# Ordering the q work behind the value product's eviction, and the ranks of three batches in an ordinary PSUM bank

## The chip, the cores and the metric

The kernel runs on one core of one Trainium2 chip. The metric is the device time of one launch in microseconds; there is one span and one granted TensorE clock to look at.

## The reference, cut to what matters

Three stages follow each other. The first is attention over 4 batches, 8 heads, 576 positions of 64 values: `scores = q k^T / 8` under a causal mask, softmax, times `v`; a second term reads a memory matrix with `phi(q) = max(q,0) + min(exp(q),1)`, divides by its own norm, and a gate per head mixes the two. The result is cast into rows `x` of 512 values, 2304 of them.

The second stage is a mixture of 8 experts. For each row an argmax over 8 logits picks the expert, softmax gives its weight `gate_w`, and an output gate is a sigmoid:

```
h = max(x[mask] @ w1[e], 0); out[mask] = gate_w * eom * (h @ w2[e])
```

The third stage is a dense layer, `max(x @ w_in, 0)**2 @ w_out`, on all 2304 rows.

## The kernel before

**Attention.** The two heads of a pair are handled together, so there are 16 pairs (4 batches of 4). A pair goes through four stages, each a lane in one loop: *prep* (load q and k, split them into a high and a low part, DMA the parts into stacked tiles `q2`, `k2`, `qlz`), *front* (scores into PSUM, row maximum `negm` on VectorE, exponential `a` on ScalarE), *back* (TensorE transposes of `a` into `pt`, copies into `aTs`, the memory read `pm`, the value product into `pva` and `pvb`), and *end* (transposes of the value product into `ppt`, the mix `tl` and `xb`, store, transposes `pxt`, gate logits `plg`). One turn of the loop, here called a step, runs the end of one pair, the back of the next, the front of the one after, and the prep of the one after that. So a step is about one pair's work on each engine, and four pairs are in flight.

The order on each engine is not written out. The program is traced lane by lane, and a scheduler with a timeline of its own then picks, engine by engine, which ready instruction comes next. Each engine executes its instructions in that order; what one needs from another is a semaphore wait. The context `tc.issue_after(ins)` adds only an ordering rule for that scheduler: what is traced inside it is placed behind `ins` on the same engine. It adds no wait on the chip by itself.

The lines around the change: L171 evicts PSUM tiles, among them `pvs<-pva` on ScalarE, remembered as `c.value`. L188 casts `kh`, L198 to L200 compute `qh`, `ex`, `rq` on ScalarE from the loaded tile `qraw` (two buffers), L201 computes `ql` and L226 `qpad` on VectorE. L275 is the row maximum, L278 the exponential. Transposes have line L76. The score of the last 64 rows goes through `psl`, a PSUM tile of two banks of which there is one buffer (`c.wide`); other PSUM tiles come from a pool of six banks (`c.bank`).

**Routing.** After a batch's last pair, `route_batch` computes on VectorE which expert each row takes (`oh`), on TensorE each row's rank among the rows of its expert (`prank`), on VectorE again the gate's softmax (`zs`, `eo`, `sp`) and from the ranks a block and an offset (`rblk`, `roff`). The first three batches are routed inside the attention loop, the last one inside the expert stage. When three batches are known, `route_early` fills the first expert slots, so that the first rows and weights can be fetched while the last pairs of attention still run.

**Experts and dense layer** run behind it in an order that is largely written out, and are not touched.

Of the kernel before, what the change touches and what calls it, by code (L numbers as in the profile page):

```python
# [12 lines left out]
I32 = mybir.dt.int32  # L13
U32 = mybir.dt.uint32
AF = mybir.ActivationFunctionType
ALU = mybir.AluOpType
AX = mybir.AxisListType
# [4 lines left out]
B, H, S, D = 4, 8, 576, 64  # L22
# [3 lines left out]
NB = 5  # L26
# [110 lines left out]
def attention(tc, c, q, k, v, x_dram, pools):  # L137
    nc = tc.nc
# [34 lines left out]
    def pair(b, hp, lgT):  # L173
# [6 lines left out]
        def load(nm, src, pool, nb):  # L180
            t = pool.tile([P, S], F32, tag=nm + "raw", name=nm + "raw", bufs=nb)
            nc.sync.dma_start(out=t, in_=src[b, hp])
            return t

        ks = load("k", k, fr, 3)
        qs = load("q", q, fr, 2)
# [7 lines left out]
        ql = fr.tile([P, S], F32R, tag="ql", name="ql", bufs=1)  # L194
        ex = fr.tile([P, S], F32, tag="ex", name="ex", bufs=1)
        rq = fr.tile([P, S], F32, tag="rq", name="rq", bufs=1)
        with tc.issue_after(c.value.ins) if c.value and b == 0 else nullcontext():
            nc.scalar.mul(qh, qs, 0.125)  # L198
        nc.scalar.activation(ex, qs, AF.Exp)
        nc.scalar.activation(rq, qs, AF.Relu)  # L200
        nc.vector.scalar_tensor_tensor(out=ql, in0=qs, scalar=0.125, in1=qh.bitcast(F32), op0=ALU.mult, op1=ALU.subtract)  # L201
        stacked = b or hp >= NPLAIN

# [237 lines left out]

    order = list(pairs())
    gens = [pair(*o) for o in order]
    n = len(gens)

# [71 lines left out]
def route_batch(tc, c, b, wk):  # L517
    nc = tc.nc
    cs = slice(b * NB, (b + 1) * NB)
    sh = (P, NB, E)  # L520
    lg, lo = c.lg[:, cs, 0:E], c.lg[:, cs, E:2 * E]
    oh = c.oh[:, cs]

    def t3(name):
        return wk.tile([P, NB, E], F32, tag=name, name=name, bufs=1)

    def t2(name, dt=F32):
        return wk.tile([P, NB], dt, tag=name, name=name, bufs=1)

    mx, m2, zs, so = t2("mx"), t2("m2"), t2("zs"), t2("so")  # L530
    dd, eo = t3("dd"), t3("eo")
    tt = c.tt[b % 2]
    tx = tt[:, :, 0:E]
    nc.scalar.activation(eo, lo, AF.Exp, scale=-1.0)
    nc.vector.tensor_reduce(out=mx, in_=lg, axis=AX.X, op=ALU.max)
    mxb = mx.unsqueeze(2).to_broadcast(sh)
    yield "f"
    nc.vector.tensor_tensor(out=tx, in0=lg, in1=mxb, op=ALU.is_equal)
    nc.vector.tensor_sub(dd, lg, mxb)
    yield "f"  # L540
    nc.vector.tensor_mul(tx, tx, c.edv)
    yield "f"
    nc.scalar.activation(dd, dd, AF.Exp)
    nc.vector.tensor_reduce(out=m2, in_=tt, axis=AX.X, op=ALU.max)
    yield "f"
    nc.vector.tensor_tensor(out=oh, in0=tx, in1=m2.unsqueeze(2).to_broadcast(sh), op=ALU.is_equal)
    yield "q"
    pr = c.wide("prank")
    pv = pr[:, 0:NB * E]
    ohf = oh.rearrange("p j e -> p (j e)")  # L550
    nc.tensor.matmul(pv, lhsT=c.ones, rhs=c.cum[:, b:b + 1].to_broadcast((P, NB, E)), start=True, stop=False)
    nc.tensor.matmul(pv, lhsT=c.tri, rhs=ohf, start=False, stop=False)
    for j in range(1, NB):
        nc.tensor.matmul(pr[:, j * E:NB * E], lhsT=c.ones, rhs=ohf[:, 0:(NB - j) * E], start=False, stop=j == NB - 1)
    if b == B - 1:
        pt = c.tot = pr[:, 512:512 + E]
        nc.tensor.matmul(pt, lhsT=c.ones, rhs=c.cum[:, B - 1], start=True, stop=False)
        for j in range(NE_COL, NCOL):
            nc.tensor.matmul(pt, lhsT=c.ones, rhs=c.oh[:, j], start=False, stop=j == NCOL - 1)
    yield "f"  # L560
    nc.vector.tensor_reduce(out=zs, in_=dd, axis=AX.X, op=ALU.add)
    nc.vector.tensor_scalar_add(eo, eo, 1.0)
    yield "f"
    nc.vector.tensor_scalar_add(zs, zs, 1e-9)
    nc.vector.reciprocal(eo, eo)
    yield "f"
    nc.vector.reciprocal(zs, zs)
    nc.vector.tensor_mul(eo, eo, oh)
    yield "f"
    nc.vector.tensor_reduce(out=so, in_=eo, axis=AX.X, op=ALU.add)  # L570
    yield "f"
    nc.vector.tensor_mul(zs, zs, so)
    for i in range(3):
        yield "f"
        nc.vector.tensor_copy(c.sp[:, i, cs], zs)
        if i < 2:
            yield "f"
            nc.vector.tensor_sub(zs, zs, c.sp[:, i, cs])
    yield "f"
    rk = t3("rk")  # L580
    rs = t2("rs", I32)
    nc.vector.tensor_mul(rk, pv.rearrange("p (j e) -> p j e", j=NB), oh)
    yield "f"
    with nc.allow_low_precision("whole numbers"):
        nc.vector.tensor_reduce(out=rs, in_=rk, axis=AX.X, op=ALU.add)
    yield "f"
    nc.vector.tensor_single_scalar(c.rblk[:, cs], rs, 7, op=ALU.logical_shift_right)
    nc.vector.tensor_single_scalar(c.roff[:, cs], rs, P - 1, op=ALU.bitwise_and)
    yield "f"
    nc.vector.tensor_tensor(out=c.ohoff[:, cs], in0=c.ioff.unsqueeze(1).to_broadcast((P, NB, P)),  # L590
                            in1=c.roff[:, cs].unsqueeze(2).to_broadcast((P, NB, P)), op=ALU.is_equal)
    if b < B - 1:
        sm = wk.tile([P, E], F32, tag="sm", name="sm", bufs=1)
        nc.vector.tensor_reduce(out=sm, in_=oh.rearrange("p j e -> p e j"), axis=AX.X, op=ALU.add)
        nc.vector.tensor_add(c.cum[:, b + 1], c.cum[:, b], sm)
# [700 lines left out]
def body(tc, q, k, v, M, z, beta, wg, w1, w2, w_in, w_out, out, dbg=None):  # L1296
# [3 lines left out]
    with ExitStack() as top:  # L1300
# [18 lines left out]
        with ExitStack() as st:  # L1319
            e = st.enter_context  # L1320
            fr = e(tc.tile_pool(name="fr", bufs=2, reuse_waits="tile"))
            aw = e(tc.tile_pool(name="aw", bufs=2, reuse_waits="tile"))
            at = e(tc.tile_pool(name="at", bufs=2, reuse_waits="tile"))
            wk = e(tc.tile_pool(name="wk", bufs=2, reuse_waits="tile"))
            ld = e(tc.tile_pool(name="ld", bufs=4, reuse_waits="tile"))
            per = e(tc.tile_pool(name="per", bufs=1, reuse_waits="tile"))
            c.setup = lambda: route_consts(tc, c, rt, x_dram)
            c.memory = (wg, M, z, beta)
            c.route = lambda b: route_batch(tc, c, b, rt)
            c.route_early = route_early(tc, c, cpool, rt)  # L1330
            with tc.manual_schedule(engines=AMAN) if AMAN else nullcontext():
                tail = attention(tc, c, q, k, v, x_dram, (fr, ld, wk, aw, at, per, lt))
            if dbg == "attn":
                for _ in tail:
                    pass
                nc.sync.dma_start(out=out, in_=x_dram[0:N, 0:DM])
                return
# [57 lines left out]
```

## Time and profile before

| | us |
|---|---|
| median of 3 runs | 913.57 (913.28 to 913.73) |
| the profiled execution | 913.89 |
| its span | 912.2 |
| TensorE busy in the span | 891.9 (98%) |
| TensorE weight loads | 727.3 (80%) |
| VectorE busy | 558.4 (61%) |
| ScalarE busy | 469.7 (51%) |

The span is the profiled execution without 1.7 us around it. Attention takes the first 235 us or so, the experts go to about 510 us, the dense layer to the end. Matmuls are pipelined and their ends modelled, so a busy TensorE says that it had work, not that it ran at its best; its idle time, on the other hand, is time in which nothing was ready.

### The profile page before, as it was taken

The page shows a single profiled execution, that of the slowest core. Times are in us where ns is not written, and L with a number is a line of the kernel's source. Part 1 is how long each engine was busy: PE and PEld are TensorE (multiplying, and loading weights), DVE is VectorE, ACT ScalarE, POOL GpSimd, SP SyncE. Part 2 cuts the span into 40 slices and gives each one's busy share as a digit, 9 for nine tenths or more (in the row PEclk, how much of TensorE's full clock was granted, in tenths as well). Part 3 has the DMA queues.
Part 4 walks back from the last instruction along what each step waited for, and adds up shares of the span by engine and source line. Part 5 has one row for each costly group of instructions (what it writes and reads, how often), then busy time and mean ns, then how long its engine had stood idle before and what let it go on. Part 6 is the DMA issues. An engine that isn't in the chain of part 4 may idle for free. (4 is left out here: it accounts for less than half of the span.)

```text
span 912.2 us, 14430 instructions
## 1 busy us (share of the span) xinstructions
PE 891.9 (98%) x5208; PEld 727.3 (80%) x5208; DVE 558.4 (61%) x1083; ACT 469.7 (51%) x934; POOL 191.1 (21%) x265
## 2 busy tenths in 40 slices
PE   8899999999989999999999999999999999999998
PEld 5677777777557889889898788888888888888897
DVE  7787988887586887786778699332223222222232
ACT  6788787864445765566566578432222222222232
POOL 6234233423002133054413004130002000100000
PEclk8999999999999999999999999999999999999999
DMA  7987778655647978856761674120002000100010
GB/s 202 219 196 191 192 191 208 157 134 176 202 152 260 353 284 294 295 195 195 247 239 70 238 238 172 35 93 12 12 12 70 1 1 1 46 1 1 3 44 24
DMA packets 81932, 128.97 MB, mean 141 GB/s; under 512 B 9473, under 2 KB 34049, under 8 KB 81857
## 3 DMA queue, kind: packets, MB, share of 16 engines
q1 hardware_dynamic: 76144, 108.86, 39.1%
q0 software_dynamic: 5712, 19.14, 6.4%
q8 instruction: 43, 0.70, 0.3%
q14 instruction: 33, 0.26, 0.1%
HBM read 109.10 MB, written 15.99 MB: 137 GB/s over the span
## 5 line engine op out<-in xcount | busy, mean ns | idle before, releaser
L1232 DVE SCALAR_TENSOR_TENSOR r<-phf,r 128x512 f32<-128x512 f32 (+1 forms) x64 | 40.0, 625 | 176.9 <-ACT r L1230 176.9
L1230 ACT ACTIVATE r<-phf 128x512 f32<-128x512 f32 (+1 forms) x79 | 43.8, 554 | 185.9 <-PE phf L82 181.6
L886 DVE TENSOR_TENSOR wc<-raw,wc 128x1024 fp32r<-128x1024 f32 x91 | 118.3, 1343 | 14.4 <-ACT wc L884 12.9
L80 PE MATMUL phf<-yT,w 128*128 128x512 f32 (+1 forms) x320 | 119.9, 375 | 0.0
L82 PE MATMUL phf<-yT,w 128*128 128x512 f32 (+1 forms) x320 | 118.2, 369 | 1.0 <-DVE w L1140 1.0
L81 PE MATMUL phf<-yT,w 128*128 128x512 f32 (+1 forms) x320 | 117.9, 369 | 0.0
L884 ACT CAST wc<-raw 128x1024 fp32r<-128x1024 f32 x108 | 106.3, 1056 | 18.9 <-DMA raw<-in_w_dram 5.3
L80 PE MATMUL po<-w,gT 128*128 128x512 f32 x256 | 99.8, 391 | 0.3 <-PEq L1102 0.3
L81 PE MATMUL po<-w,gT 128*128 128x512 f32 x256 | 99.8, 390 | 0.0
L82 PE MATMUL po<-w,gT 128*128 128x512 f32 x256 | 92.8, 391 | 0.0
L278 ACT ACTIVATE a<-sc,negm 128x512 f32<-128x512 f32 (+3 forms) x128 | 66.6, 529 | 12.8 <-DVE negm L275 12.8
L80 PE MATMUL py<-wc,hT 128*128 128x512 f32 x176 | 69.9, 397 | 0.2 <-ACT hT L923 0.2
L81 PE MATMUL py<-wc,hT 128*128 128x512 f32 x176 | 68.9, 392 | 0.8 <-DVE wc L886 0.8
L82 PEld LDWEIGHTS phf<-yT,w 128*128 128x128 f32 x320 | 60.2, 188 | 11.7 <-DVE w L1140 1.4
L80 PEld LDWEIGHTS phf<-yT,w 128*128 128x128 f32 x320 | 60.2, 188 | 11.5
L82 PE MATMUL py<-wc,hT 128*128 128x512 f32 x176 | 68.9, 391 | 0.4 <-DVE hT L924 0.4
L81 PEld LDWEIGHTS phf<-yT,w 128*128 128x128 f32 x320 | 60.3, 188 | 10.1
L1237 DVE TENSOR_TENSOR gT<-r,gT 128x512 fp32r<-128x512 f32 x63 | 43.5, 691 | 40.2 <-ACT gT L1236 39.8
L275 DVE TENSOR_REDUCE negm<-sc 128x1 f32<-128x512 f32 (+3 forms) x128 | 55.2, 484 | 19.2 <-PE sc L272 19.1
L886 POOL TENSOR_TENSOR wc<-raw,wc 128x1024 fp32r<-128x1024 f32 x17 | 44.2, 2600 | 90.2 <-ACT wc L884 82.5
L80 PEld LDWEIGHTS po<-w,gT 128*128 128x128 f32 x256 | 48.1, 188 | 10.8 <-issue 0.7
L82 PEld LDWEIGHTS po<-w,gT 128*128 128x128 f32 x256 | 48.0, 188 | 10.3
(358 smaller groups left out, 1953.4 us busy)
## 6 DMA issues: line engine op xcount, KB each, us to landing
raw<-in_w_dram SPq DMA_DIRECT2D x64, 1024.0 KB, 5.4
q<-qh SPq DMA_DIRECT2D x60, 128.0 KB, 2.6
kraw<-in_k_dram SPq DMA_DIRECT2D x16, 288.0 KB, 5.3
qraw<-in_q_dram SPq DMA_DIRECT2D x16, 288.0 KB
vts<-in_v_dram SPq DMA_DIRECT2D x16, 256.0 KB, 3.5
x_dram<-xb SPq DMA_DIRECT2D x16, 256.0 KB, 4.6
k<-kh SPq DMA_DIRECT2D x30, 128.0 KB, 3.2
k<-kl SPq DMA_DIRECT2D x30, 128.0 KB, 2.5
```

What stands on the lines that cost most here:

```text
L80: nc.tensor.matmul(out, lhsT=lh, rhs=rh, start=start, stop=False)
L81: nc.tensor.matmul(out, lhsT=lh, rhs=rl, start=False, stop=False)
L82: return nc.tensor.matmul(out, lhsT=ll, rhs=rh, start=False, stop=stop)
L275: nc.vector.tensor_reduce(out=negm[:, h, j:j + 1], in_=psv, axis=AX.X, op=ALU.max, negate=True)
L278: nc.scalar.activation(a[:, h, aoff[j]:aoff[j] + nk], psv, AF.Exp, bias=negm[:, h, j:j + 1], accum_out=ssum[:, h, j:j + 1])
L884: nc.scalar.copy(wc[:, 0, ks], raw[:, ks])
L886: eng.tensor_sub(wc[:, 1, ks], raw[:, ks], wc[:, 0, ks].bitcast(F32))
L1230: nc.scalar.activation(r[:, 0:nt], ph[:, 0:nt], AF.Relu)
L1232: nc.vector.scalar_tensor_tensor(out=r[:, 0:nt], in0=ph[:, 0:nt], scalar=0.0, in1=r[:, 0:nt], op0=ALU.max, op1=ALU.mult)
L1237: nc.vector.tensor_sub(gT[:, 1, 0:nt], r[:, 0:nt], gT[:, 0, 0:nt].bitcast(F32))
```

## The change

First, all three ScalarE operations on q are placed behind the latest traced eviction of the value product, for every batch. Before, this held for `qh` alone and only in the first batch. Second, the ranks of the first three batches get an ordinary bank in place of the two-bank buffer, and are read before the gate's softmax. The last batch keeps the two-bank tile, since it needs a second region in it, and reads it where it did.

```diff
-        with tc.issue_after(c.value.ins) if c.value and b == 0 else nullcontext():
+        with tc.issue_after(c.value.ins) if c.value else nullcontext():
             nc.scalar.mul(qh, qs, 0.125)
-        nc.scalar.activation(ex, qs, AF.Exp)
-        nc.scalar.activation(rq, qs, AF.Relu)
+            nc.scalar.activation(ex, qs, AF.Exp)
+            nc.scalar.activation(rq, qs, AF.Relu)
...
-    pr = c.wide("prank")
+    pr = c.wide("prank") if b == B - 1 else c.bank("prank")
...
+    def ranks():
+        nc.vector.tensor_mul(rk, pv.rearrange("p (j e) -> p j e", j=NB), oh)
+        yield "f"
+        with nc.allow_low_precision("whole numbers"):
+            nc.vector.tensor_reduce(out=rs, in_=rk, axis=AX.X, op=ALU.add)
+        yield "f"
+
+    yield "f"
+    if b < B - 1:
+        yield from ranks()
     nc.vector.tensor_reduce(out=zs, in_=dd, axis=AX.X, op=ALU.add)
...
-    nc.vector.tensor_mul(rk, pv.rearrange("p (j e) -> p j e", j=NB), oh)
...
-        nc.vector.tensor_reduce(out=rs, in_=rk, axis=AX.X, op=ALU.add)
...
+    if b == B - 1:
+        yield from ranks()
```

ScalarE, around the eviction of the fourth pair's value product (the step that starts near 70 us); `qraw_1154` is the q of the pair being prepared, `qraw_1356` that of the pair behind it:

```order
 L278 ACTIVATE a_962,ssum_961<-sc11_1042,negm_960 128x256
 L278 ACTIVATE a_962,ssum_961<-sc11_1042,negm_960 128x128
+L171 COPY pvs1_119<-pva_1097 128x448
 L198 ACTIVATE qh_1178<-qraw_1154 128x576
-L199 ACTIVATE ex_1382<-qraw_1356 128x576
-L200 ACTIVATE rq_1383<-qraw_1356 128x576
-L171 COPY pvs1_119<-pva_1097 128x448
+L199 ACTIVATE ex_1180<-qraw_1154 128x576
+L200 ACTIVATE rq_1181<-qraw_1154 128x576
 L188 CAST kh_1156<-kraw_1152 128x576
 L278 ACTIVATE a_962,ssum_961<-sc20_1119,negm_960 128x384
```

The eviction moves ahead of the three q operations, and `ex` and `rq` now belong to the same pair as `qh`, not to the one behind it; between the eviction and the exponential of `sc20` stand four operations where there was one.

VectorE in the same step (`sc_1119` and `sc_1120` are the scores whose exponentials ScalarE computes next):

```order
 L355 TENSOR_TENSOR xm<-pm_1091,cm 128x256
-L201 SCALAR_TENSOR_TENSOR ql<-qraw,qh 128x576
 L171 COPY pvs_119<-pvb 128x128
 L407 TENSOR_TENSOR lgT<-lgT,plg 128x160
+L201 SCALAR_TENSOR_TENSOR ql<-qraw,qh 128x576
 L275 TENSOR_REDUCE negm<-sc_1119 128x1
 L275 TENSOR_REDUCE negm<-sc_1120 128x1
 L381 TENSOR_TENSOR tl<-ppt_1132,cl 128x512
 L381 TENSOR_TENSOR tl<-ppt_1140,cl 128x128
+L226 SCALAR_TENSOR_TENSOR qpad_115<-ex,rq 128x576
 L171 COPY aTs_128<-ptl 128x2x2x64
```

`ql` moves behind the eviction of `pvb` and the logits, directly ahead of the row maximum, and `qpad` comes in behind `tl`.

TensorE in the step that starts near 83 us, the last before the first batch is ranked:

```order
 L76 MATMUL ppt_1342<-ident,pvs_118 128x128
 L76 MATMUL ptl<-ident,al 128x128 x4
-L76 MATMUL pt_1405<-ident,a 128x128 x4
+L76 MATMUL pt_1405<-ident,a 128x128 x2
+L80 MATMUL psl<-kh,qlasth_122 128x288
+L76 MATMUL pt_1405<-ident,a 128x128 x2
 L76 MATMUL pt_1411<-ident,a 128x128 x3
 L254 MATMUL sc_1416<-k_1192,q_1193 128x512
```

Before, this step had no `psl` product, since the ranks held its buffer, and the next step had two; now every step has one, in the place it has in the others.

## Rows read from the trace of the kernel before

**Rows 1.** Stretches: length, busy PE, PEld, DVE, ACT, POOL (instructions), clock, DMA share, GB/s.
```profile
44.02:57.73 13.71, 12.53 (x108) 9.96 (x106) 10.56 (x27) 11.04 (x32) 4.66 (x10) 1.00 0.80 204
57.73:70.23 12.50, 12.50 (x108) 9.94 (x106) 10.24 (x27) 10.42 (x32) 4.65 (x10) 1.00 0.81 199
300.00:320.00 20.00, 19.29 (x134) 17.41 (x134) 18.43 (x21) 15.68 (x22) 4.07 (x2) 1.00 0.99 347
```
**Rows 2.** TensorE in order of time: start, us, operation [idle before <-releaser].
```profile
32.48 0.66 PE L76 MATMUL ppt<-ident,pvs 128*128 128x128 f32 x4 [2.19 <-ACT pvs L171]
46.84 0.66 PE L76 MATMUL ppt<-ident,pvs 128*128 128x128 f32 x4 [1.18 <-ACT pvs L171]
85.14 0.66 PE L76 MATMUL ppt<-ident,pvs 128*128 128x128 f32 x4 [0.82 <-ACT pvs L171]
103.48 0.37 PE L80 MATMUL psl<-kh,qlasth 128*128 128x288 f32 x1 [0.50 <-ACT al L288]
107.81 2.70 PE L363 MATMUL pva<-aTs,vts 128*64 128x448 f32 x20 [0.55 <-DVE xTg L171]
150.81 0.66 PE L76 MATMUL ppt<-ident,pvs 128*128 128x128 f32 x4 [1.05 <-ACT pvs L171]
```
**Rows 3.** ScalarE in order of time, first full step.
```profile
30.75 0.68 ACT L199 ACTIVATE ex<-qraw 128x576 f32<-128x576 f32 x1 [2.93 <-DMA qraw<-in_q_dram]
...
31.91 0.51 ACT L171 COPY pvs<-pva 128x448 f32<-128x448 f32 x1
32.32 0.68 ACT L198 ACTIVATE qh<-qraw 128x576 fp32r<-128x576 f32 x1
32.91 0.66 ACT L188 CAST kh<-kraw 128x576 fp32r<-128x576 f32 x1
33.47 0.58 ACT L278 ACTIVATE a<-sc,negm 128x384 f32<-128x384 f32 x1
```
**Rows 4.** ScalarE in an even step, 121 to 129 us.
```profile
121.60 0.69 ACT L198 ACTIVATE qh<-qraw 128x576 fp32r<-128x576 f32 x1
122.18 0.69 ACT L199 ACTIVATE ex<-qraw 128x576 f32<-128x576 f32 x1
122.75 0.69 ACT L200 ACTIVATE rq<-qraw 128x576 f32<-128x576 f32 x1
123.33 0.54 ACT L171 COPY pvs<-pva 128x448 f32<-128x448 f32 x1
124.55 0.67 ACT L188 CAST kh<-kraw 128x576 fp32r<-128x576 f32 x1 [0.69 <-PE sc L267]
125.22 0.58 ACT L278 ACTIVATE a<-sc,negm 128x384 f32<-128x384 f32 x1
...
128.49 0.69 ACT L278 ACTIVATE a<-sc,negm 128x512 f32<-128x512 f32 x1 [0.83 <-DVE negm L275]
```
**Rows 5.** TensorE in the same step.
```profile
120.27 2.70 PE L363 MATMUL pva<-aTs,vts 128*64 128x448 f32 x20
...
123.12 0.48 PE L403 MATMUL plg<-xTg,wg 128*32 128x160 f32 x8
```
**Rows 6.** TensorE's weight loads in the same step.
```profile
125.94 0.53 PEld L76 LDWEIGHTS pt<-ident,a 128*128 128x128 f32 x5 [0.17 <-ACT a L278]
```
**Rows 7.** ScalarE in a step where no q work is left.
```profile
199.81 0.53 ACT L171 COPY pvs<-pva 128x448 f32<-128x448 f32 x1 [2.10 <-PE pva L363]
202.10 0.58 ACT L278 ACTIVATE a<-sc,negm 128x384 f32<-128x384 f32 x1 [1.76 <-DVE negm L275]
```
**Rows 8.** VectorE: `ql` at three places, and the row maxima before 202.10 us.
```profile
14.50 1.54 DVE L201 SCALAR_TENSOR_TENSOR ql<-qraw,qh 128x576 fp32r<-128x576 f32 x1
...
94.75 0.75 DVE L201 SCALAR_TENSOR_TENSOR ql<-qraw,qh 128x576 fp32r<-128x576 f32 x1
...
122.39 0.82 DVE L201 SCALAR_TENSOR_TENSOR ql<-qraw,qh 128x576 fp32r<-128x576 f32 x1 [0.17 <-ACT qh L198]
...
201.51 1.02 DVE L275 TENSOR_REDUCE negm<-sc 128x1 f32<-128x384 f32 x2
```
**Rows 9.** GpSimd beside the first `ql` of the group above.
```profile
14.03 1.40 POOL L191 TENSOR_TENSOR kl<-kraw,kh 128x576 fp32r<-128x576 f32 x1 [1.85 <-ACT kh L188]
```

More of the change, by code (lines that the diff above doesn't have):

```diff
@@ L559, in route_batch @@
             nc.tensor.matmul(pt, lhsT=c.ones, rhs=c.oh[:, j], start=False, stop=j == NCOL - 1)
+    rk = t3("rk")
+    rs = t2("rs", I32)
+    def ranks():
[4 more added lines that the diff above has]
+        yield "f"
     yield "f"
+    if b < B - 1:
+        yield from ranks()
     nc.vector.tensor_reduce(out=zs, in_=dd, axis=AX.X, op=ALU.add)
@@ L579, in route_batch @@
     yield "f"
-    rk = t3("rk")
-    rs = t2("rs", I32)
-    nc.vector.tensor_mul(rk, pv.rearrange("p (j e) -> p j e", j=NB), oh)
-    yield "f"
-    with nc.allow_low_precision("whole numbers"):
-        nc.vector.tensor_reduce(out=rs, in_=rk, axis=AX.X, op=ALU.add)
-    yield "f"
+    if b == B - 1:
+        yield from ranks()
     nc.vector.tensor_single_scalar(c.rblk[:, cs], rs, 7, op=ALU.logical_shift_right)
```

## The prediction, as made before the run

> **What bounds the kernel now.** I read the stretches first, a step of the attention loop each. An even step (57.73 to 70.23) takes 12.50 us and TensorE is busy in all of it; the step before takes 13.71 with the same 108 matmuls [rows 1]. So TensorE sets a step's length, and what it waits is added to it: 13.71 - 12.50 = 1.21, and the one wait in that step is 1.18 [rows 2]. The granted clock is 1.00, full speed, in both.
>
> Next the list of TensorE's waits between 28 and 212 us. Four of the six are for the eviction `pvs` on ScalarE: 2.19 + 1.18 + 0.82 + 1.05 = 5.24 us [rows 2]. The other two, 0.50 and 0.55, are in one step, the one with two `psl` products; together 6.29.
>
> ScalarE in order of time says why the eviction is late. At 30.75 `ex` starts after 2.93 us of waiting for a load of q, and the eviction behind it in the queue starts only at 31.91 [rows 3]. The order shows whose q that is: `ex` and `rq` run a pair ahead of `qh`, on a tile whose load has just been issued.
>
> Last, the even step itself, to see how much room there is in it. `qh`, `ex` and `rq` run from 121.60 to 123.33 [rows 4], while TensorE computes the value product, which ends at 120.27 + 2.70 = 122.97 [rows 5]. They fill a hole in which ScalarE has nothing else: where no q work is left, it waits 2.10 us for that product and evicts 0.05 after its end [rows 7]. Then come `kh` at 124.55 and the exponential `a` at 125.22 [rows 4]; TensorE's transposes of `a` start at 125.94 after 0.17 of idle time, released by that exponential [rows 6]. So in an even step the path from eviction through `kh` to `a` has already no slack: what delays `a` delays TensorE.
>
> **The change part by part.** *What goes.* In the new order `ex` uses the q of the pair in hand, loaded a step ahead, so the wait for the load goes in all steps but the first, where `qh` now needs the same tile that `ex` waited for until 30.75. With the eviction ahead of it, none of the four `ppt` waits has its cause left.
>
> *What comes in its place.* Behind the eviction now stand `qh`, `ex`, `rq`, `kh`, and only then `a`. ScalarE is free at 121.60 and has nothing to do before 122.97 + 0.05 = 123.02, where the eviction starts. From there, by the distances between starts: eviction to `qh` 0.41 (31.91 to 32.32) [rows 3]; `qh` to `ex` 0.58, `ex` to `rq` 0.57, `rq` to the next 0.58 [rows 4]; `kh` to `a` 0.56 [rows 3]. Sum 2.70, so `a` starts at 125.72, not 125.22. I call this rise r = 0.50 a step. `kh` had waited 0.69 for TensorE's score product; that wait is now filled with q work, but only that much of the 1.73 us of it.
>
> VectorE does not decide it: `ql` (0.82) [rows 8] now runs from about 0.1 after `qh` ends, 123.43 + 0.69 + 0.1 = 124.22, to 125.04, and the maximum follows. From the start of the maximum to `a` it is 0.59 (201.51 to 202.10) [rows 7, 8], which gives 125.63, before 125.72.
>
> TensorE's transposes then wait 0.17 + 0.50 = 0.67 in every step with q work. There are 12 such steps, starting at 44.02 to 187.61, after the first full one. The order of TensorE's work between `ppt` and `a` is the same as before in the even steps, so it brings nothing to fill this.
>
> *The ranks.* The bank takes no instruction away; it moves a `psl` product one step earlier, about 0.9 us less in one step and more in its neighbour, at nothing in the sum, since TensorE is full in both. What it does remove are the 0.50 and the 0.55. The reading of the ranks ahead of the softmax issues the same two instructions. But the routing operations now all stand ahead of the row maximum for two batches, as they already did for the third. There the maximum starts 201.51 - 199.81 = 1.70 after the eviction [rows 7, 8]; with `ql` (0.75) [rows 8] in that queue it is 2.45, and `a` 2.45 + 0.59 = 3.04 after the eviction in place of 2.70. That is 0.34 more in two steps. With one bank of six held by the ranks, a wait for a bank could arise in three steps; the trace has none, the nearest row is the 0.50 for `psl`, so 0 to 1.5 us in all. I take 0, since the bank is read about as soon as the ranks are there.
>
> *The sum.* Eight even steps: 8 x 0.50 = +4.00. Late steps: 0.67 - 1.18 = -0.51 and 0.67 - 0.82 = -0.15. Ranked steps: 0.67 + 0.34 - 1.05 = -0.04, twice (the first loses 0.50 + 0.55, the second 1.05). First step: `qh` at 30.75, then 0.58 + 0.57 + 0.58 + 0.56 puts `a` at 33.04, not 33.47 [rows 3]: -0.43. In all +2.83 us, or 12r - 3.17.
>
> On the profiled execution's 913.89 that is 916.7; the median of the runs is 0.32 lower, so I give 916.4.
>
> *Does it reach the end?* Expert weights are chosen by the routing at the end of attention, so the load stream starts later by as much. In 300 to 320 us the DMA share is 0.99 with TensorE at 19.29 of 20 [rows 1]: two limits close together, both behind attention. I carry the whole of it.
>
> *Bounds of r.* From below 0: if the exponential is not what holds the transposes, nothing is added and 12r - 3.17 leaves -3.2, or 910.4. From above: `qpad` moves behind `tl`, where GpSimd computes `kl`. An operation of that kind took 1.54 us at 14.50 instead of 0.75 [rows 8] while `kl` ran from 14.03 to 15.43 [rows 9]. Of the 0.79, ScalarE has some slack at the next maximum (0.83 in the even step [rows 4], of which I count half, 0.42, because the added work has used the rest). That leaves 0.37 and r = 0.87: +7.3, or 920.8.
>
> The Trainium skill has the rule for this, in "SBUF — State Buffer", section "Who interferes with whom": a VectorE operation with two SBUF inputs needs a port pair it shares with GpSimd, and whoever issues first holds it for the whole instruction. The row at 14.50 agrees with it: 1.54 us beside `kl`. By the rule in full, every `qpad` would wait for the rest of `kl`; by the even step, where `ql` takes 0.82 beside GpSimd's copies, the price is small.
>
> **The rivals.** *Faster: the late eviction was the whole loss.* Speaks for it: all of TensorE's named waits have this cause or the `psl` buffer, and TensorE has weight loads and a pipeline that may cover 0.5 us. Then r is 0 and the time 910.4; with the first step's wait gone too it would be 913.6 - 6.3 = 907.3. Against it: the transposes in the even step are already released by `a`. Chance 0.21.
>
> *No difference.* r between 0.11 and 0.42 keeps the sum within 1.83 us, 0.2% of the time, which is about what a measurement of this kernel tells from none; or the expert stage's loads absorb a part. 911.7 to 915.4; middle value 913.6. Chance 0.27.
>
> *Slower by more: the port.* `qpad` against `kl` in each of 12 steps, from the point where `kl` is still running when `tl` ends; 918.8 to 920.8. For it the two rows; against it that `kl` begins only after `kh`, at about 125.9, and with 1.4 us of work has 0.4 left when `tl` ends near 126.9. Chance 0.12.
>
> **How the numbers follow.** My forecast, r from 0.42 to 0.63, gives 915.4 to 918.0 and has 0.40; 916.4 is its value. Slower holds 0.40 + 0.12 = 0.52, same 0.27, faster 0.21. The range runs from r = 0 to just short of the port's worst, 910.4 to 920.0.
>
> **What would show it.** In the new profile the four `ppt` waits on `pvs` should be gone except in the first step, and no `ex` waits for a load. ScalarE should sit idle for 1.4 us before each eviction, released by `pva`, with `qh` 0.41 behind it. The weight loads of `pt` should wait about 0.67 us for `a` in twelve steps, and an even step should take 13.0 us. I am wrong if those waits are under 0.3 us, if the even step stays at 12.5, or if the eviction starts well before 0.05 behind its product, which can't be. The `psl` wait of 0.50 should be gone; if a wait for a bank stands in its place, the ranks hold it too long.

## The result, and the profile after

The changed kernel takes 925.19 us (924.21 to 926.54), the kernel before 913.65 in the same runs: a ratio of 1.0127, with a 95% interval of 1.0110 to 1.0145. It is slower by 11.5 us; forecast were 2.8, and 920.0 was the upper end of the range. The profiled execution took 924.21, its span is 922.5, and the granted clock is 0.996 in both. Times are medians of fast executions: one slow execution of `both_off` (4413 us) is left out, with which its median is the 917.85 that a later expectation names.

Nearly all of it is in attention. The last `plg` (the gate logits, which start each step) starts at 243.83 us instead of 233.81, 10.0 later, and the span is longer by 10.3. The list of stretches shows an even step (columns as in [rows 1]):

```profile
125.46:138.88 13.42, 12.96 (x109) 10.03 (x107) 11.25 (x26) 10.47 (x32) 5.18 (x9) 1.00 0.76 192
```

That is 13.42 where [rows 1] have 12.50 and the forecast had 13.0, again at full clock. The forecast for ScalarE comes out nearly to the digit. In order of time (start, us, operation, idle time before it and its releaser):

```profile
125.36 0.53 ACT L171 COPY pvs<-pva 128x448 f32<-128x448 f32 x1 [1.30 <-PE pva L363]
125.79 0.69 ACT L198 ACTIVATE qh<-qraw 128x576 fp32r<-128x576 f32 x1
126.37 0.68 ACT L199 ACTIVATE ex<-qraw 128x576 f32<-128x576 f32 x1
126.95 0.67 ACT L200 ACTIVATE rq<-qraw 128x576 f32<-128x576 f32 x1
127.52 0.66 ACT L188 CAST kh<-kraw 128x576 fp32r<-128x576 f32 x1
128.09 0.58 ACT L278 ACTIVATE a<-sc,negm 128x384 f32<-128x384 f32 x1
...
132.35 0.69 ACT L278 ACTIVATE a<-sc,negm 128x512 f32<-128x512 f32 x1 [1.26 <-DVE negm L275]
```

ScalarE idles 1.30 before the eviction and `a` starts 2.73 behind it (forecast 2.70; in [rows 4] 1.89). No `ex` waits for a load, and none of the four `ppt` waits of [rows 2] is left. But the last line is new: the 512-wide exponential starts 6.89 after the step's `plg` at 125.46; in [rows 4, 5] it was 128.49 - 123.12 = 5.37. TensorE's lists, matmuls first, then weight loads, show what waits for it:

```profile
125.46 0.48 PE L403 MATMUL plg<-xTg,wg 128*32 128x160 f32 x8
...
128.33 0.37 PE L80 MATMUL psl<-kh,qlasth 128*128 128x288 f32 x1 [0.16 <-ACT kh L188]
133.19 0.45 PE L254 MATMUL sc<-k,q 128*128 128x256 f32 x2 [0.19 <-ACT a L278]
```
```profile
128.30 0.19 PEld L80 LDWEIGHTS psl<-kh,qlasth 128*128 128x128 f32 x1 [0.36 <-POOL qlastl L214]
128.81 0.53 PEld L76 LDWEIGHTS pt<-ident,a 128*128 128x128 f32 x5 [0.32 <-ACT a L278]
...
133.18 0.30 PEld L254 LDWEIGHTS sc<-k,q 128*128 128x128 f32 x2 [0.34 <-ACT a L278]
```

These two matmuls show only 0.35 us of idle time, and the whole step 13.42 - 12.96 = 0.46; the ends of matmuls are modelled. The weight loads show 0.36 + 0.32 + 0.34 = 1.02 where [rows 6] had 0.17. The difference of 0.85 is nearly the 0.92 by which the step is longer. The first two, 0.68, are the forecast's 0.67, split between `psl`, whose matmul waits for `kh` in the same queue, and `pt`. The third was not in the forecast. The product of the smaller scores has no input from that exponential, which reads a PSUM bank; so what it waits for is taken here to be that bank.

Why the exponential is late stands in VectorE's and GpSimd's lists of the same step, after the change and then, in the even step of [rows 4, 5], before it:

```profile
128.24 0.87 DVE L381 TENSOR_TENSOR tl<-ppt,cl 128x512 f32<-128x512 f32 x2
129.04 1.31 DVE L226 SCALAR_TENSOR_TENSOR qpad<-ex,rq 128x576 f32<-128x576 f32 x1
130.27 0.41 DVE L171 COPY aTs<-ptl 128x256 f32<-128x256 f32 x1
130.61 0.92 DVE L340 SCALAR_TENSOR_TENSOR cl<-ssum,gneg 128x10 f32<-128x10 f32 x1
...
131.69 1.23 DVE L275 TENSOR_REDUCE negm<-sc 128x1 f32<-128x512 f32 x2
```
```profile
128.32 1.42 POOL L191 TENSOR_TENSOR kl<-kraw,kh 128x576 fp32r<-128x576 f32 x1 [0.27 <-POOL qlastl L214]
129.69 2.23 POOL L383 TENSOR_TENSOR xb<-tl,xm 128x512 f32<-128x512 f32 x2
```
```profile
126.69 0.16 DVE L340 SCALAR_TENSOR_TENSOR cl<-ssum,gneg 128x10 f32<-128x10 f32 x1
...
127.77 1.29 DVE L275 TENSOR_REDUCE negm<-sc 128x1 f32<-128x512 f32 x2 [0.66 <-PE sc L272]
```
```profile
126.74 1.70 POOL L383 TENSOR_TENSOR xb<-tl,xm 128x512 f32<-128x512 f32 x2
```

`qpad` runs while `kl` runs, and takes 1.31 us; the median of its 16 rows before is 0.75. Then `xb` takes 2.23 instead of 1.70; then `cl`, ten values per row, takes 0.92 instead of 0.16. The maximum behind them starts 6.23 after the step's `plg`. In the even step before it was 4.65 (127.77), after a wait of 0.66 for TensorE's product; here it waits for nothing but the queue ahead of it.

### The profile page after: what moved, and what is told of

Same layout as the page of the kernel before. It is cut to its first block, busy times and chain, and to the rows that moved or that the text cites. A ratio compares the mean times of both kernels' runs of the same rounds, so it can differ in the third digit from the quotient of the medians.

```text
span 922.5 us, 14438 instructions
## 1 busy us (share of the span) xinstructions
PE 899.3 (97%) x5208; PEld 728.0 (79%) x5208; DVE 569.4 (62%) x1083; ACT 468.7 (51%) x934; POOL 197.4 (21%) x265
```

## The experiments

### The two halves alone

`q_only` is the first part of the change, `ranks_only` the second.

```diff
-        with tc.issue_after(c.value.ins) if c.value and b == 0 else nullcontext():
+        with tc.issue_after(c.value.ins) if c.value else nullcontext():   # q_only, with ex and rq inside
...
-    pr = c.wide("prank")
+    pr = c.wide("prank") if b == B - 1 else c.bank("prank")               # ranks_only, read early
```

> Only the first part of the change: the three ScalarE operations on q behind the eviction, the ranks as before in the two-bank tile and read late. Theory A (the queue on ScalarE and what follows from it cost everything): 924 to 927 us, steps of 13.4 us without routing, `a` 2.6 us behind the step boundary; the ranks' part only takes back the two waits of 0.50 and 0.55. Rival B (a good part of the 11.5 us comes from the ranks' bank and the early reading): 916 to 920 us.

> Only the second part: ranks of three batches in an ordinary bank and read ahead of the gate's softmax; q work as before. Theory A: 912.3 to 914.3 us, the two waits of 0.50 and 0.55 gone (-1.05), up to 0.7 lost to a later row maximum. Rival B (the bank or the early reading costs): 917 to 921 us, with a new wait for a bank or for `negm` in the three steps with routing.

Measured: 924.04 for `q_only`, ratio 1.0110 (1.0095 to 1.0125); 918.04 for `ranks_only`, 1.0056 (1.0039 to 1.0073). Neither theory had both. The q part alone makes nearly the whole loss, but the ranks' part, which the forecast had at -0.37 (-0.50 - 0.55 + 2 x 0.34), costs some 5 us by itself. The two don't add up: together they cost 1.27%, not 1.66%.

### `qpad` beside `kl`

`qpad_late` leaves ScalarE's order as in the changed kernel and moves `qpad` behind the 512-wide maxima, the last of which is remembered as `c.max512`:

```diff
-        nc.vector.scalar_tensor_tensor(out=qpad[i3][:, 0:S], in0=ex, ...)
...
+        with tc.issue_after(c.max512.ins) if c.max512 else nullcontext():
+            nc.vector.scalar_tensor_tensor(out=qpad[i3][:, 0:S], in0=ex, ...)
         psl = wide("psl")
```

> The changed kernel with `qpad` placed behind the maxima of the 512-wide scores on VectorE, so that it no longer runs beside `kl`; ScalarE's order stays. Theory P (0.4 us of each step's 0.93 comes from `qpad` beside `kl`, which takes 1.31 instead of 0.75 us and makes the 512-wide maximum late): `qpad` 0.75 us, no wait of TensorE for `a` ahead of the scores of rows 128 and 256, steps of 13.0 us, 919.5 to 921.5. Theory Q (all of it is the queue on ScalarE, from eviction to `kh` and `a`): steps stay at 13.4, 924 to 926.

Measured: 921.53, ratio 1.0088 (1.0073 to 1.0103), and even steps of 13.00 us, as theory P had it. `qpad` is back at its old duration, and of the three waits of the weight loads the first two are left:

```profile
128.32 1.29 DVE L274 TENSOR_REDUCE negm<-sc 128x1 f32<-128x512 f32 x2 [0.60 <-PE sc L271]
129.53 0.75 DVE L282 SCALAR_TENSOR_TENSOR qpad<-ex,rq 128x576 f32<-128x576 f32 x1
```
```profile
126.01 0.19 PEld L80 LDWEIGHTS psl<-kh,qlasth 128*128 128x128 f32 x1 [0.34 <-POOL qlastl L214]
126.53 0.53 PEld L76 LDWEIGHTS pt<-ident,a 128*128 128x128 f32 x5 [0.33 <-ACT a L278]
```

0.34 + 0.33 = 0.67 is the forecast's figure, and 13.00 its step. So an even step's +0.92 is 0.50 of queue on ScalarE and 0.42 of `qpad`'s place.

This run takes `qpad`'s own 0.75 us out of the queue as well, so by itself it does not show that the waiting beside GpSimd is the cause. The rows above settle that as an estimate: without the excess of 0.56 (`qpad`) and 0.76 (`cl`), 1.32 together, the maximum would start 4.91 after the step's `plg` with `qpad` still in its place, near the 4.65 of before. ScalarE's wait for it was 1.26, and TensorE's wait behind that 0.34.

`exrq` separates the two from the other side. It is the kernel before with `ex` and `rq` alone placed behind the eviction; `qh` stays free to run ahead of it.

```diff
         with tc.issue_after(c.value.ins) if c.value and b == 0 else nullcontext():
             nc.scalar.mul(qh, qs, 0.125)
+        with tc.issue_after(c.value.ins) if c.value else nullcontext():
-        nc.scalar.activation(ex, qs, AF.Exp)
-        nc.scalar.activation(rq, qs, AF.Relu)
+            nc.scalar.activation(ex, qs, AF.Exp)
+            nc.scalar.activation(rq, qs, AF.Relu)
```

> Of the kernel before, only `ex` and `rq` behind the eviction of the value product; `qh` free to run ahead of it, ranks as before. So two operations stand between the eviction and `kh`, and they end about when `kh` may start. Theory Q (the three operations in the queue delay `a`): without `qh` there is no delay of `a`; with the load wait gone the even step stays at 12.5 us and the time is 909 to 911. Theory P (`qpad` beside `kl`): `qpad` now stands between the row maximum and `tl`, right where `kl` starts, takes 1.3 us, and makes `tl`, `xb` and the 512-wide maximum late: even step 12.9 to 13.1, 914 to 918.

Measured: 925.9, ratio 1.0143 (1.0126 to 1.0160): as slow as the changed kernel or slower, with a shorter queue on ScalarE. It lies outside both expectations; theory P had the direction and too small a size. VectorE, GpSimd and the weight loads in an even step:

```profile
130.23 1.87 DVE L227 SCALAR_TENSOR_TENSOR qpad<-ex,rq 128x576 f32<-128x576 f32 x1
132.02 0.87 DVE L382 TENSOR_TENSOR tl<-ppt,cl 128x512 f32<-128x512 f32 x2
```
```profile
130.08 1.41 POOL L191 TENSOR_TENSOR kl<-kraw,kh 128x576 fp32r<-128x576 f32 x1 [2.34 <-issue]
```
```profile
130.60 0.53 PEld L76 LDWEIGHTS pt<-ident,a 128*128 128x128 f32 x5 [0.17 <-ACT a L279]
132.75 0.19 PEld L255 LDWEIGHTS sc<-k,q 128*128 128x128 f32 x1 [0.56 <-DVE tl L382]
...
135.74 0.30 PEld L255 LDWEIGHTS sc<-k,q 128*128 128x128 f32 x2 [0.40 <-ACT a L279]
```

The wait of `pt` for `a` is 0.17, as in [rows 6]: the queue on ScalarE costs nothing here. The other two waits are new and come from VectorE, for `tl` behind `qpad` and for the late 512-wide maximum.

`qpad` is issued 0.15 after `kl` begins instead of 0.72, and takes 1.87 instead of 1.31. It ends 0.61 after `kl`'s end in both (132.10 - 131.49, and 130.35 - 129.74), so it waits for the rest of `kl` and then does its work. `kl` itself takes 1.41 or 1.42 in both, and `tl` beside it, with one input in PSUM (128.24 in the changed kernel), 0.87 as in the row at 132.02, where `kl` has ended. The Trainium skill, "SBUF — State Buffer", section "Who interferes with whom", says that a VectorE instruction with two SBUF inputs contends with a GpSimd instruction that reads SBUF. By the same section the shared port pair is an exclusive lock, and the order of issue decides which of the two waits. The traces agree with both. The price of `qpad` is what was left of the other's 1.41, less 0.14 us: 0.70 left and 0.56 paid, 1.26 left and 1.12 paid, and for `ql` in [rows 8, 9] 0.93 left and 0.79 paid.

### The ranks: the bank or the early reading?

`bank_only` keeps the late reading, `early_only` the two-bank tile. `dummy` is the kernel before with a further bank taken at the place of the ranks.

```diff
+    pr = c.wide("prank") if b == B - 1 else c.bank("prank")   # bank_only
...
+    if b < B - 1:                                             # early_only, pr = c.wide("prank")
+        yield from ranks()
...
+    if b < B - 1:                                             # dummy, ranks as before
+        dm = c.bank("dummy")
+        nc.tensor.matmul(dm[:, 0:E], lhsT=c.ones, rhs=c.cum[:, b], start=True, stop=True)
...
+    if b < B - 1:
+        dr = wk.tile([P, E], F32, tag="dr", name="dr", bufs=1)
+        nc.vector.tensor_copy(dr, dm[:, 0:E])
```

> The kernel before with the ranks of three batches in an ordinary bank, but read where they were read before, behind the gate's softmax. Theory B (the bank costs: `prank` holds one of six from its first product to its reading, and `pm`, `sc` and `pt` then wait for another): 917 to 920 us, at least the 918.0 of bank and early reading together, since the bank is held longer. Theory E (the early reading costs, since it puts two more operations ahead of the row maximum): 911.5 to 913.5.

> The kernel before with the ranks read ahead of the gate's softmax, but in the two-bank tile as before. Theory B (the bank costs): 912.5 to 914.5 us. Theory E (the early reading costs): 916.5 to 919.

> The kernel before, with one more ordinary bank taken at the place of the ranks: one small product into it ahead of the ranks' own, and one small VectorE copy out of it where the ranks are read. The ranks stay in the two-bank tile, so `psl` stays where it was. Theory B1 (what costs is that five banks are left for a stretch): waits of `pm` for `lg` and of `sc` for `tl` or `a` appear in the steps with routing, 915.5 to 918.5 us. Theory B2 (what costs is the `psl` product that moves into the step before): 913 to 914.5.

Measured: `bank_only` 918.37, ratio 1.0058 (1.0043 to 1.0073); `early_only` 913.58, 1.0006 (0.9993 to 1.0018). So it is the bank, and the early reading costs nothing that can be measured. TensorE's list in two steps of `ranks_only` has waits for one:

```profile
145.55 0.68 PE L349 MATMUL pm<-mbd,qpad 128*128 128x130 f32 x4 [0.29 <-DVE lg L430]
154.29 0.50 PE L254 MATMUL sc<-k,q 128*128 128x512 f32 x1 [0.28 <-DVE tl L381]
158.31 0.45 PE L254 MATMUL sc<-k,q 128*128 128x256 f32 x2 [0.74 <-ACT a L278]
```

None of the releasers computes an input of what waits; each reads a tile in one of the six banks. Over the three batches these waits are 0.29 x 3 + 0.29 + 0.28 + 0.74 x 2 = 2.92 us, twice the upper bound of 1.5. They name the bank, but they don't add up to the loss: some waits for `pvs` are shorter in this run, so all of TensorE's named waits between 28 and 212 us sum to 6.00 us, against the 6.29 of before. The profiled execution is 3.8 us longer all the same, and 3.7 of that is in the six steps in which batches are routed (table below). How the missing bank turns into time there I could not assign to single rows.

`dummy` took 917.58, ratio 1.0039 (1.0024 to 1.0053), with the ranks and `psl` in their old place. So taking a bank has a price without the moved `psl` product, most of what `bank_only` shows. The waits were others than expected (`psl` for `al` 1.04 twice, `pt` for `aTs` 0.49 and 0.38); `psl` has its own buffer, so that wait is not for one of the six banks. Whether the missing bank causes it directly, or the order that the scheduler makes of it, is not shown.

`bank_short` should have shortened the time for which the bank is held, by issuing the product of the running counts last:

```diff
-    nc.tensor.matmul(pv, lhsT=c.ones, rhs=c.cum[:, b:b + 1].to_broadcast((P, NB, E)), start=True, stop=False)
-    nc.tensor.matmul(pv, lhsT=c.tri, rhs=ohf, start=False, stop=False)
+    nc.tensor.matmul(pv, lhsT=c.tri, rhs=ohf, start=True, stop=False)
...
+    nc.tensor.matmul(pv, lhsT=c.ones, rhs=c.cum[:, b:b + 1].to_broadcast((P, NB, E)), start=False, stop=True)
```

> Ranks of three batches in an ordinary bank and read early, with the product of the running counts (`cum`) issued last in place of first. So the bank is taken only when `oh` is ready, and held for a shorter time than the 6 us or so from 144.5 to the reading behind 150.6 in the run of the ranks' part alone (918.0). Theory B1 (time with five banks): the wait of `pm` for `lg` goes, 914 to 916.5. Theory B2 (the moved `psl` product): unchanged, 917.5 to 919.

Measured: 924.18, ratio 1.0118 (1.0103 to 1.0133), which neither had. The product that needs `oh` now stood first in TensorE's order, and TensorE waited 2.09 us for `oh` in each of three steps; behind two of these waits the clock fell as well (last section). It says nothing on the time a bank is held.

### The forecast's own sum

`both_off` is `qpad_late` with the ranks in the two-bank tile; `q_early` the changed kernel with the ranks there, and `qpad` beside `kl`. The edit is one line in both:

```diff
-    pr = c.wide("prank") if b == B - 1 else c.bank("prank")
+    pr = c.wide("prank")
```

> The changed kernel with the two costs taken away that the forecast had at nothing: `qpad` behind the 512-wide maxima (no longer beside `kl`), and the ranks in the two-bank tile, still read ahead of the gate's softmax. What is left is the q work behind the eviction, that is the forecast's own sum. Theory S (the forecast failed in these two terms and in nothing else): 916 to 918 us, steps of 13.0 us, no new waits in the steps with routing. Rival R (the q work itself costs more than the 0.5 us a step of the forecast): 920 or more.

> The changed kernel with the ranks in the two-bank tile again, still read ahead of the gate's softmax; `qpad` stays beside `kl`. Theory O (the waits for a bank lie under those that the port makes, so the bank is worth little here): 923 to 925 us, within 1.5 of the changed kernel's 925.2, and some 6 above the run with `qpad` late and the two-bank tile (917.85). Rival (the costs add): 920.5 to 921.5, that is 925.2 less the 3.7 to 4.5 of the bank.

Measured: `both_off` 917.67, ratio 1.0043 (1.0030 to 1.0057), even steps of 13.0. This is the kernel that the forecast's sum describes, and 916.4 was its time. `q_early` 924.31, ratio 1.0131 (1.0116 to 1.0147): not to be told from the changed kernel's 1.0127. So, in order: q work behind the eviction +0.43%, `qpad` beside `kl` on top of it +0.88%, the bank on top of both nothing that can be measured, though it costs 0.56% in the kernel before. Without the port it costs about 0.45% (1.0088 against 1.0043). Theory O expected this; which wait covers which I have not traced row by row.

The profiles show where each of these costs lies. The table has the change against the kernel before, in us, from one start of `plg` to the next: the six steps in which batches are routed (before, they start at 82.70, 95.77, 135.64, 147.96, 187.61 and 199.91), and the seven between 44.02 and 187.61 that are not among them.

| | seven steps without routing | six with routing |
|---|---|---|
| forecast | +2.49 | +0.77 |
| `both_off` | +2.47 | -0.29 |
| `qpad_late` (bank taken) | +2.41 | +2.65 |
| `q_early` (`qpad` beside `kl`) | +5.24 | +3.67 |
| changed kernel (both) | +4.93 | +5.52 |
| `ranks_only` | +0.14 | +3.68 |
| `dummy` | -0.56 | +3.98 |

Without the two terms the seven steps come out as forecast. In these profiles the bank costs only where batches are routed. `qpad` beside `kl` costs 0.4 a step where they are not, and 4.0 us in the six where they are. In the first step of each of those pairs `q_early` has no `psl` product between the transposes and the smaller scores, and TensorE waits there for the late exponential longer than the 0.15 to 0.19 us of the steps without routing:

```profile
92.33 0.45 PE L254 MATMUL sc<-k,q 128*128 128x256 f32 x2 [0.93 <-ACT a L278]
```

### The load wait alone

`pin` takes away the wait of [rows 3] without the eviction rule. `pin_early` adds the early reading. `qraw3` instead gives the loaded q a third buffer, `qraw3_early` adds the early reading to that, and `qraw3_pin0` adds to `qraw3_early` the rule of `pin` in the first batch.

```diff
+            qi = nc.scalar.mul(qh, qs, 0.125)                 # pin
+        with tc.issue_after(qi.ins):
+            nc.scalar.activation(ex, qs, AF.Exp)
+            nc.scalar.activation(rq, qs, AF.Relu)
...
-        qs = load("q", q, fr, 2)
+        qs = load("q", q, fr, 3)                              # qraw3
```

> The kernel before with one rule alone: `ex` and `rq` behind `qh` of the same pair, with nothing placed behind the eviction. So they use a q loaded a step ahead, and the three fill the hole ahead of the eviction as before. Theory A (the load wait and the late evictions are one loss, the queue behind the eviction another): the four waits of TensorE for `pvs` go, 5.24 us, the even step stays at 12.5: 908 to 910.5. Rival (the q operations pass the end of the value product, so the eviction stays late): 912 to 915.

> `ex` and `rq` behind `qh` of the same pair, as in the run that did that alone (914.0), and the ranks read ahead of the gate's softmax, in the two-bank tile. Theory L (in the steps with routing the last rows' product `psl` waited 1.4 us twice because `prank` held its buffer till it was read): buffer free earlier, at least one of the two waits gone, 911 to 913. Rival (it waits for the exponential `al` on ScalarE, held up by the routing operations on VectorE, wherever the ranks are read): 913.5 to 915.5.

> The kernel before with a third buffer for the loaded q, order rules as before. Theory L (the late evictions come from `ex` waiting for a q load that could not be issued earlier): the load is issued a step earlier, the four waits of TensorE for `pvs` (5.24 us) go or shrink, 908.5 to 911.5. Rival (the evictions are late for other reasons too, or the wait moves elsewhere): 912.5 to 914.5.

> A third buffer for the loaded q and the ranks read early in the two-bank tile; nothing behind the eviction. If the two add: the waits of 0.46 for `al` and 0.55 for `xTg` in two steps go (-2.0 against the third buffer alone, 911.6): 909 to 910.5 us. If the order in the steps with routing decides otherwise: 911 to 913.

> The same with `ex` and `rq` behind `qh` of the same pair in the first batch, where the first step's `ex` still waits for a q that was issued late (2.80 us for `pvs` at 32.26). If that wait is the loss: another 0.7 to 1.5 us less than the run without it, 908 to 909.5. Rival: the wait of `psl` for `kh` that the rule showed at 33.1 us in every step (1.7) takes its place, no difference.

Measured: `pin` 914.02, ratio 1.0011 (1.0000 to 1.0023), `pin_early` 913.75, 1.0006 (0.9997 to 1.0015): the rival's time, both times. For `pin` it came for another reason than the rival gave, since the evictions are no longer late: the four `ppt` waits are gone and the steps without routing take 12.45 to 12.52. But in their place TensorE's list has

```profile
33.13 0.37 PE L80 MATMUL psl<-kh,qlasth 128*128 128x288 f32 x1 [1.70 <-ACT kh L188]
37.97 0.45 PE L255 MATMUL sc<-k,q 128*128 128x256 f32 x2 [0.30 <-ACT a L279]
102.08 0.37 PE L80 MATMUL psl<-kh,qlasth 128*128 128x288 f32 x1 [1.43 <-ACT al L289]
156.23 0.37 PE L80 MATMUL psl<-kh,qlasth 128*128 128x288 f32 x1 [1.42 <-ACT al L289]
```

These are 4.85 us against the 5.24, with a lower clock behind one of them (below). `pin_early` has the two waits for `al` unchanged, so reading the ranks early does not free them.

`qraw3` took 911.63, ratio 0.9986 (0.9977 to 0.9995): the `ppt` waits of 1.18, 0.82 and 1.05 are gone, the first remains (2.80), and the two small ones (0.46 for `al`, 0.55 for `xTg`) now stand in two steps with routing, where the kernel before had them in one. The time is between the two expectations. It is the only version whose interval lies wholly below the kernel before, by 0.14%, about 1.3 us. `qraw3_early` (911.61, 0.9988, 0.9977 to 1.0000) and `qraw3_pin0` (911.89, 0.9994, 0.9984 to 1.0004) add nothing to it that can be measured; both came out as their rivals had it.

## Why the prediction was wrong

**What was right.** The direction; that TensorE sets the step and that nothing behind attention absorbs a delay (10.0 of the 10.3 us are there by its end). The queue on ScalarE: 2.70 forecast, 2.73 measured; TensorE's wait 0.67 and 0.68; the step 13.0 forecast, and 13.00 in `qpad_late`, where nothing else is left. With the two terms below taken away the sum of +2.8 met +3.9 (2.7 to 5.2). That the sums meet is in part luck: in the profile of `both_off` the seven steps without routing are as forecast, but the first step ended 1.82 us later and not 0.43 earlier. There TensorE waited 2.76 us for `kh`, and from 35 to 38 us its granted clock was 0.50, that is 1.2 GHz.

**The step that failed first: r, that is the bounds of r and the port's chance.** The forecast set `qpad` beside `kl` at nothing, 12% likely and at most 0.37 a step. Its reason, "that `kl` begins only after `kh`, at about 125.9, and with 1.4 us of work has 0.4 left", had the place right (2.78 behind `plg` by the forecast, 2.86 measured) and the price wrong. The remainder was 0.70 us (129.74 - 129.04). And the wait was counted once, while it goes back and forth: `qpad` waits for `kl`, `xb` for `qpad`, `cl` for `xb`, 0.56 + 0.76 us on VectorE ahead of the maximum. Half of ScalarE's wait of 0.83 was taken as slack, where what counts is the maximum itself, 6.23 after `plg` and not 4.65. Last, I looked for the damage at the maximum only, not at the bank that the exponential holds from the next score product. By the runs this is +0.88% instead of 0. The bound of 0.37 was close for an even step (0.42); with the measured r of 0.92 the forecast's own 12r - 3.17 would have given 921.4. Most of the rest of the miss is in the steps with routing, which the forecast took for even or late steps or priced at -0.04: +0.77 in all, where `qpad` beside `kl` alone makes them +3.67 and both terms +5.52.

The row that would have told is in the trace before, in a step with routing. VectorE and GpSimd:

```profile
98.29 1.38 DVE L572 TENSOR_TENSOR zs<-zs,so 128x5 f32<-128x5 f32 x1
```
```profile
98.23 1.42 POOL L191 TENSOR_TENSOR kl<-kraw,kh 128x576 fp32r<-128x576 f32 x1 [2.09 <-issue]
```

Five values per row in 1.38 us, where the same form took 0.15 at 102.47: that is the 1.36 that was left of `kl`. It was in [rows 8, 9] too, where the forecast took only the 0.79 from it: `ql` ended at 14.50 + 1.54 = 16.04, that is 0.61 behind `kl`'s end at 15.43, the same 0.61 as in the two runs above.

**The second: the bank at 0, bounds 0 to 1.5.** "The trace has none" was no reason for 0: what five banks do can't be read from a trace with six. Nor does it hold. The wait of `pva` for `xTg` at 107.81 in [rows 2] is of the kind found in `ranks_only`: `xTg` is no input of `pva`, and its copy reads one of the six banks. The forecast put it down to `psl`. Alone it costs 0.56% (0.39 to 0.73), some 5 us. The forecast's argument, that the bank is read about as soon as the ranks are there, overlooked that it is taken by the first product, the one on the running counts: in `ranks_only` TensorE issued it at 144.47 and the next one at 150.56. That this length is what costs is not shown, since `bank_short` failed to test it. In the changed kernel this error is covered by the first, so the size of the miss is the port's.

**The gain and the small terms.** The four waits went, as forecast; in the first step a wait of 1.30 us of `psl` for `kh` came instead. The 0.34 for the ranks read early can't be seen (`early_only`). The first step came 0.89 earlier, not 0.43, but over the profiles of all these kernels its end (the first `plg` of the table's steps) lies between 42.97 and 45.84 us, so neither figure says much. The `psl` wait of 0.50 went too, and waits of the kind found in `ranks_only` stood in its place (`pm` for `lg`, 0.22 or 0.23 in each batch), as the last part of the prediction named.

## What to carry to other kernels

Ahead of moving a VectorE operation with two SBUF inputs, look at what GpSimd runs at its new place, and charge it with the whole remainder of that instruction, then the next one on GpSimd with what it was held up; the trace of before shows the price in tiny operations that take over a microsecond. Two inputs may not be the only case: the cast `sp` of five values per row, with one input, took 0.85 us at 100.82 in the kernel before, while `xb` ran, and 0.17 at 103.35. A buffer taken from a pool that hardly waited is not free: bound it by the waits of the tiles that share the pool. And if an operation waits for a load, one more buffer for the load is the edit to try ahead of a new order: here it gained 0.14%, and the new order alone lost 0.43%.

## What the runs showed of the hardware

Behind a wait of 1.43 us in the middle of full work TensorE ran at half clock for a while. In `pin`, stretches of 1 us (columns as in [rows 1]):

```profile
101.00:102.00 1.00, 0.00 (x0) 0.00 (x0) 1.00 (x5) 0.90 (x3) 0.00 (x0) 1.00 0.95 213
102.00:103.00 1.00, 0.92 (x8) 0.88 (x8) 1.00 (x3) 1.00 (x3) 0.18 (x1) 1.00 0.94 194
103.00:104.00 1.00, 1.00 (x8) 0.94 (x8) 0.83 (x3) 1.00 (x4) 0.00 (x0) 0.61 0.99 276
104.00:105.00 1.00, 1.00 (x7) 0.96 (x6) 0.87 (x4) 0.14 (x2) 0.00 (x0) 0.50 0.74 129
...
106.00:107.00 1.00, 1.00 (x8) 1.00 (x7) 0.64 (x2) 1.00 (x4) 0.28 (x2) 0.68 0.00 0
```

Here the granted clock falls to 0.50, 1.2 GHz, when TensorE has been at work again for about 1 us, and the matmuls at 103.25 then take 0.63 us in place of 0.39. The step takes 16.94 us; the other step with the same order and a wait of 1.42 kept the full clock and took 15.30. So this wait cost 1.6 us more than it shows, and the other did not; `pin_early` has the same pair, 16.93 and 15.29. In `bank_short`, of the waits of 2.09, those that end at 149 and 203 us were followed by a clock of 0.50 and the one that ends at 94 us was not; nor was the wait of 2.19 in the kernel before. In `qraw3` the clock was already 0.50 when TensorE came back from its wait of 2.80. What decides between them the runs don't tell.
